# Attention's plan with a count of SP's transfer queue and new offsets, and a state factor from summed angles

## The chip, the cores and the metric

The kernel runs on one core of one Trainium2 chip. The metric is the device time of one execution in microseconds, as the median of several runs. The profile is one further execution of the same program, recorded by the hardware profiler; its span goes from the first to the last instruction.

The engines are called PE (TensorE, matrix products), DVE (VectorE), ACT (ScalarE), POOL (GpSimd) and SP (SyncE, which here only issues DMA transfers).

## What is computed

Three stages follow one another. A gated linear attention with a complex decay per channel, a mixture of experts with a greedy capacity-bound assignment, and a gated linear unit:

```python
# attention: B, H, S, D = 4, 8, 768, 48
mag = sqrt(a_re**2 + a_im**2)
scale = minimum(mag, 0.999) / (mag + 1e-6)
a_re_n, a_im_n = a_re * scale, a_im * scale
for t in range(S):                      # state S_re, S_im: D x D per head
    new_re = ar * S_re - ai * S_im
    new_im = ar * S_im + ai * S_re
    S_re, S_im = new_re + outer(k[t], v[t]), new_im
    y[t] = q[t] @ S_re
# experts: N, D, E, F = 3072, 384, 8, 1024; cap = N // E
#   tokens go to experts in the order of their logits, cap each
out[mask_e] = relu(x[mask_e] @ w1[e]) @ w2[e]
# unit: (x @ w_a) * (x @ w_b) @ w_out, 384 -> 1536 -> 384
```

## The kernel before

**Attention** works on chunks of 128 positions. There are 6 chunks and 4 batches; a pass (`i`, 0 to 11) handles one chunk `c = i // 2` of two batches at once, as tiles of 128 positions by 768 columns (two batches, eight heads, 48 channels). For each pass `gates` loads a_re, a_im, q, k and v and turns the decay into a logarithm `e` of its size and an angle `th`. `sums` forms the running sums along the chunk by matmul with a triangular matrix: `LL` for the sizes (with a rounded part `n` that VectorE computes and TensorE subtracts again) and `HH` for the angles, of which `r` keeps the part within one turn. `turned` takes sines of `r` (`s`, then squared, and `sn`) and turns k and q with them into `nat`. `unit` (one per batch) transposes `nat` (`TT`), forms the scores (`S`), the outer products of the state (`X`), the output (`Y`) and the router's logits (`O`).

The state passes from chunk to chunk through `factor`: for a pass `i` of two or more it builds, on 16 rows by 48 columns, the size and the cosine and sine of the turn from the last position of chunk `i - 2` to the last of chunk `i`. Its inputs are single rows of tiles, moved by SP into `fw` (lines 363 and 448): the last row of `s` and `sn` of pass `i - 2`, the first row of `s` and `sn` of pass `i`, the first row of `e` and `th`, and rows of `ea` into `ends`. Twelve VectorE instructions (lines 477 to 497) and three ScalarE instructions (469 to 473) make the factor; TensorE transposes it (line 503) and ScalarE copies it to `pb`. VectorE multiplies the state `xs` with it into `rta` and `rtb` (line 513), SP swaps the two halves of `rtb` into `sw` (two transfers, lines 517 and 518), and VectorE adds `rta` and `sw` to the state `Sb` (line 521). That state enters `Y` (line 587) and, with the outer product, the next `xs` (line 570).

**The order of the work** is fixed before the program is built, by `Plan`. Every step is a task with an engine, an assumed duration, what it reads and writes, and a due time (22 per pass). `order` lays the tasks out with a list scheduler: at each step it takes the engine and the task that can start earliest, and among those the one with the lowest rank. The rank is the due time times `STRETCH`, less the assumed length of the chain behind it in the same due time (`tail`), plus an offset `EARLIER` by kind (engine letter and name of the tile written, as `Sre` for SP's transfer of a_re or `Aln` for ScalarE's logarithm). A change of ScalarE's function table adds `SWITCH` to the rank and 1.3 us to the time, and is held back by `PATIENCE` while less than `ENOUGH` of work waits for that table. `land` is the time from the end of a transfer's issue to its landing:

```python
t["tail"] = t["dur"] + t["land"] + HOP[t["eng"]] + max(own, default=0.0)
t["rank"] = t["due"] * STRETCH - t["tail"] + EARLIER.get(t["kind"], 0.0)
```

The engines then run their instructions in that order and wait for each other by semaphores. SP issues its transfers in order too. The two pair banks of PSUM (`NPAIR = 2`) hold `LL`, `HH` and `TT`; `SPLIT_PAIRS` limits how many pairs `LL` and `HH` hold at once. `SINGLE = 1`: the first pass is done in two halves.

**Behind attention** the router (`make_router`, `route`, `lists`) assigns tokens to the first expert, and then `moe_glu` runs the eight experts with the unit, each expert's routing beside the products of the one before.

Of the kernel before, what the change touches and what calls it, by code (L numbers as in the profile page):

```python
# [16 lines left out]
OP = mybir.AluOpType  # L17
# [17 lines left out]
SWITCH = 61.0  # L35
# [12 lines left out]
PATIENCE = 7  # L48
ENOUGH = 21.5
# [7 lines left out]
class Plan:  # L57
# [8 lines left out]
    def add(self, eng, dur, fn, reads=(), writes=(), due=0.0, take=None, drop=None, table=None, land=0.0):  # L66
        t = dict(n=len(self.tasks), eng=eng, dur=dur * SLOW if eng == "P" else dur, fn=fn, due=due, take=take, drop=drop, table=table, land=land,
# [21 lines left out]
    def order(self):  # L89
# [30 lines left out]
        while any(waiting.values()):  # L120
# [71 lines left out]
def attention(tc, q, k, v, a_re, a_im, wg, x_dram, consts, L, guard, router, glu, late):  # L192
# [8 lines left out]
    with ExitStack() as st:  # L201
# [26 lines left out]
        for nm, x in (("one", 1.0), ("shift", LIFT), ("tiny", LN(2.0e-6)), ("quarter", HALF_PI)):  # L228
# [88 lines left out]
        def gates(i, due):  # L317
# [5 lines left out]
            load, land = (2.3, 2.2) if i < 2 else (0.6, 3.8)  # L323
            for us in parts(i):
# [3 lines left out]
                for nm, t, src in (("re", ld_re, a_re), ("im", ld_im, a_im)):  # L328
                    plan.add("S", took(load, us), lambda t=t, src=src, r=r, at=at, d2=d2: SP.dma_start(t[j][:, r], flat(src, at, d2)),
                             writes=[(nm, j, u) for u in us], due=due - 20 - 40 * (i < 2), land=land)  # L330
            for x, src in ((0, q), (1, k)):
                plan.add("S", load, lambda x=x, src=src: SP.dma_start(ld_qk[j][:, x], flat(src, base, dims)),
                         writes=[("qk", j, x)], due=due - 10, land=land)
            plan.add("S", load, lambda: SP.dma_start(vb[j].rearrange("p u h d -> p (u h) d")[:, :, 0:D], flat(v, base, dims)),
                     writes=[("v", j)], due=due - 4, land=land)
# [1323 lines left out]
```

## Time and profile before

| | us |
|---|---|
| median of 3 runs | 1066.19 |
| lowest, highest run | 1063.6, 1066.37 |
| the profiled execution | 1064.48 |
| its span | 1062.9 |
| PE busy, share of the span | 994.7 (94%) |
| DVE busy | 640.8 (60%) |
| ACT busy | 501.8 (47%) |
| POOL busy | 164.6 (15%) |
| mean granted clock of TensorE | 0.975 |

Busy times are sums over stages with different limits, so they don't tell what bounds a stage; the rows by stretch further down do. Attention fills roughly the first 287 us, and its share of DVE and ACT is far higher than that of the whole.

### The profile page before, as it was taken

How to read it: one execution, taken by the hardware profiler on the slowest of the kernel's cores; microseconds unless marked ns; L12 is line 12 of the kernel's file. 1: busy time of each engine (PE TensorE's matmuls, PEld its weight loads, DVE VectorE, ACT ScalarE, POOL GpSimd, SP SyncE). 2: the span in 40 equal slices, each digit the busy share in tenths (PEclk: the TensorE clock that was granted, in tenths of full speed). 3: DMA queues.
4: the chain of work that ended last, by engine and by line, in shares of the span. 5: the costliest groups of instructions: out<-in, count | busy, mean ns of one | idle time of the engine just before them, and what ended most of it. 6: DMA issues, size and time to landing. Idle time of an engine off the chain costs nothing. (4 is left out here: it accounts for less than half of the span.)

```text
span 1062.9 us, 17395 instructions
## 1 busy us (share of the span) xinstructions
PE 994.7 (94%) x6660; PEld 901.2 (85%) x6660; DVE 640.8 (60%) x1596; ACT 501.8 (47%) x906; POOL 164.6 (15%) x217
## 2 busy tenths in 40 slices
PE   3899999999987699999999999999999999999994
PEld 1588787888746599999989999999999999999994
DVE  4689888998677987555366355455536644333321
ACT  6799898887426773332332332243233234233221
POOL 6000000000021003203112120320311213102001
PEclk9999999999968789999999999999999999999998
DMA  9866777344145644102112110310211212201000
GB/s 170 129 120 124 121 130 135 74 89 111 42 140 166 177 143 127 53 8 96 33 38 79 42 45 1 105 52 8 90 35 42 69 47 78 76 15 45 1 2 26
DMA packets 146764, 81.90 MB, mean 77 GB/s; under 512 B 130416, under 2 KB 132336, under 8 KB 146672
## 3 DMA queue, kind: packets, MB, share of 16 engines
q1 hardware_dynamic: 134448, 41.36, 20.4%
q0 software_dynamic: 12224, 39.34, 11.6%
q8 instruction: 54, 0.88, 0.3%
q14 instruction: 38, 0.31, 0.1%
HBM read 68.04 MB, written 9.44 MB: 73 GB/s over the span
## 5 line engine op out<-in xcount | busy, mean ns | idle before, releaser
L1301 PE MATMUL mm<-yh,glu 128*128 128x384 f32 x1152 | 241.7, 344 | 0.0
L1301 PEld LDWEIGHTS mm<-yh,glu 128*128 128x128 f32 x1152 | 201.5, 189 | 2.1 <-ACT yh L1153 0.4
L1335 DVE TENSOR_TENSOR g<-mm,a_s 128x384 f32<-128x384 f32 x96 | 53.4, 556 | 154.7 <-PE mm L1301 130.4
L1301 PE MATMUL mm<-yl,glu 128*128 128x384 f32 x576 | 133.2, 338 | 0.0
L1153 ACT ACTIVATE gh<-g 128x384 fp32r<-128x384 f32 x96 | 50.4, 525 | 163.5 <-DVE g L1335 163.5
L1330 ACT ACTIVATE a_s<-mm 128x384 f32<-128x384 f32 x96 | 47.1, 491 | 151.1 <-PE mm L1301 142.7
L1301 PEld LDWEIGHTS mm<-yl,glu 128*128 128x128 f32 x576 | 103.4, 187 | 0.0
L1249 PE MATMUL acc<-glu,gh 128*128 128x384 f32 x288 | 98.4, 342 | 0.0
L1250 PE MATMUL acc<-glu,gh 128*128 128x384 f32 x288 | 96.9, 336 | 0.0
L1251 PE MATMUL acc<-glu,gl 128*128 128x384 f32 x288 | 96.7, 337 | 0.1
L1202 POOL DMA_INDIRECT raw<-moe_w_in,i x64 | 64.2, 1004 | 171.0 <-DVE w2l L1154 121.5
L1154 DVE TENSOR_TENSOR gl<-g,gh 128x384 fp32r<-128x384 f32 x96 | 53.6, 558 | 40.8 <-ACT gh L1153 39.9
L1250 PE MATMUL acc<-hl,w2h 128*128 128x384 f32 x192 | 67.0, 349 | 5.2 <-DVE hl L1276 5.2
L1249 PE MATMUL mm<-xh,w1h 128*128 128x384 f32 x192 | 67.4, 352 | 0.4 <-ACT w1h L1153 0.3
L1251 PE MATMUL acc<-hh,w2l 128*128 128x384 f32 x192 | 66.1, 344 | 0.0
L1251 PE MATMUL mm<-xh,w1l 128*128 128x384 f32 x192 | 65.1, 339 | 1.1 <-DVE w1l L1154 1.1
L1249 PE MATMUL acc<-hh,w2h 128*128 128x384 f32 x192 | 65.8, 353 | 0.2 <-ACT hh L1275 0.2
L1250 PE MATMUL mm<-xl,w1h 128*128 128x384 f32 x192 | 65.0, 339 | 0.0
L1188 POOL DMA_INDIRECT raw<-moe_w_in,i x24 | 24.2, 1008 | 253.1 <-DVE left L1062 172.5
L1153 ACT ACTIVATE w1h<-raw 128x384 fp32r<-128x384 f32 x64 | 32.7, 521 | 54.1 <-PE mm L1250 51.6
L552 PE MATMUL bank<-qkT 96*128 96x128 f32 x384 | 54.1, 286 | 3.7 <-ACT qkT L543 3.4
L1154 DVE TENSOR_TENSOR w1l<-raw,w1h 128x384 fp32r<-128x384 f32 x64 | 34.9, 552 | 36.3 <-ACT w1h L1153 29.8
(277 smaller groups left out, 2007.7 us busy)
## 6 DMA issues: line engine op xcount, KB each, us to landing
stage<-moe_w_a_in SPq DMA_DIRECT2D x13, 384.0 KB, 3.2
vb<-v_in SPq DMA_DIRECT2D x12, 384.0 KB, 5.0
ld_qk<-q_in SPq DMA_DIRECT2D x12, 384.0 KB, 4.3
ld_qk<-k_in SPq DMA_DIRECT2D x12, 384.0 KB, 5.8
x_rows<-xo POOLq DMA_DIRECT2D x24, 192.0 KB, 2.4
stage<-moe_w_b_in SPq DMA_DIRECT2D x12, 384.0 KB, 3.2
stage<-moe_w_out_in SPq DMA_DIRECT2D x12, 384.0 KB, 3.5
ld_im<-a_im_in SPq DMA_DIRECT2D x11, 384.0 KB, 5.9
```

Of the source, the lines that this page charges most:

```text
L552: PE.matmul(p[:, x], qt[0:96, 4 * h4 + x, 1], qt[0:96, 4 * h4 + x, 0], start=True, stop=True)
L1153: a = A.activation(hi, src, AF.Copy)
L1154: return a, V.tensor_tensor(lo_, src, hi, op=OP.subtract)
L1188: G.indirect_dma_start(out=raw[:, j], out_offset=None, in_=w1r, in_offset=bass.IndirectOffsetOnAxis(ap=i1[:, j:j + 1], axis=0))
L1202: G.indirect_dma_start(out=raw, out_offset=None, in_=w2r, in_offset=bass.IndirectOffsetOnAxis(ap=i2[:, f:f + 1], axis=0))
L1249: PE.matmul(p, lh, rh, start=first, stop=False)
L1250: PE.matmul(p, lh, rl, start=False, stop=False)
L1251: PE.matmul(p, ll, rh, start=False, stop=last)
L1301: PE.matmul(p, a[:, j, c], b[:, j], start=(n == 0), stop=(n == 8))
L1330: A.activation(a_s, pa, AF.Copy)
L1335: V.tensor_tensor(g, pb, a_s, op=OP.mult)
```

## The change

`Plan.add` takes a new argument `wire`: the time that a transfer keeps SP's queue busy behind its issue. `order` keeps one such clock for SP: a transfer is taken as sent when the earlier ones have left the queue, and its landing counts from there. Loads of the passes from 2 on have 2.0, those of the first two passes 0.0, swaps 0.4, the unit's weights 1.2, all others 0.1. `EARLIER`, `STRETCH`, `SWITCH`, `SPLIT_PAIRS`, `PATIENCE` and `ENOUGH` have new values.

The factor no longer takes rows of `s` and `sn` of both passes: it takes one row of `r` from each, adds the angles with that of `th`, brings the sum into one turn, and takes two sines of it. The twelve VectorE instructions become ten (`angle` 4, `size` 2, `three` 4), ScalarE's three stay three, and of four row transfers two remain. The bias `quarter` goes.

```diff
-SWITCH = 61.0
+SWITCH = 34
-SPLIT_PAIRS = 3
+SPLIT_PAIRS = 2
-EARLIER = {'Acc': -2, 'Ae': 99, 'Aea': 39, 'Afw': 11, 'Ag': -75, 'Aln': -20, 'Apb': -27, 'AqkT': 9, 'Arec': 15, 'As2': -5, 'Asf': -11, 'Ath': 58, 'Axo': 8, 'AyT': -36, 'G-': -59, 'GW': -21, 'Gconsts': 2, 'Gmasks': 51, 'Gzeros': -28, 'PF': -33, 'PHH': -2, 'PLL': -39, 'PO': 68, 'PS': -40, 'PTT': 90, 'PX': 59, 'PY': 126, 'Sends': 69, 'Sfw': 67, 'Sim': -99, 'Sqk': 72, 'Sraw': -57, 'Sre': 2, 'Ssw': -147, 'Sv': -41, 'V-': 19, 'VAb': -10, 'VS': 99, 'Ve': 29, 'Vearly': -29, 'Veb': 55, 'Vft': -4, 'Vg': -28, 'Vlg': 5, 'Vn4': -38, 'Vnat': -69, 'Vr': 33, 'Vrho': 89, 'Vrt0': -55, 'Vrt1': -13, 'Vsetup': -54, 'Vxs': -152}
-STRETCH = 3.699071
+EARLIER = {'Acc': 48, 'Ae': 17, 'Aea': -62, 'Afw': 2, 'Ag': 21, 'Aln': 213, 'Apb': -89, 'AqkT': -98, 'Arec': 89, 'As2': 53, 'Asf': 104, 'Asn': 73, 'Ath': 73, 'Axo': -339, 'AyT': -47, 'G-': -187, 'GW': 169, 'Gconsts': 370, 'Gmasks': 66, 'Gzeros': 230, 'PF': -31, 'PHH': -133, 'PLL': -104, 'PO': 106, 'PS': -2, 'PTT': -183, 'PX': -273, 'PY': 129, 'Sends': 36, 'Sfw': -102, 'Sim': 30, 'Sqk': -4, 'Sraw': 54, 'Sre': 20, 'Ssw': -293, 'Sv': 39, 'V-': -57, 'VAb': -23, 'VS': -129, 'Ve': 14, 'Vearly': -74, 'Veb': 138, 'Vft': -207, 'Vfw': 23, 'Vg': -26, 'Vlg': 5, 'Vn4': -181, 'Vnat': 18, 'Vr': 2, 'Vrho': 100, 'Vrt0': 101, 'Vrt1': 94, 'Vsetup': -169, 'Vxs': -26}
+STRETCH = 3.42
-PATIENCE = 7
-ENOUGH = 21.5
+PATIENCE = 8.0
+ENOUGH = 20.0
...
+        wire = 0.0
...
+            sent = end
+            if e == "S":
+                sent = max(end, wire)
+                wire = sent + t["wire"]
             for u in users[n]:
                 left[u] -= 1
-                ready_at[u] = max(ready_at[u], end + t["land"] + (HOP[e] if T[u]["eng"] != e else 0.06))
+                ready_at[u] = max(ready_at[u], sent + t["land"] + (HOP[e] if T[u]["eng"] != e else 0.06))
...
-            load, land = (2.3, 2.2) if i < 2 else (0.6, 3.8)
+            load, land, wire = (2.3, 2.2, 0.0) if i < 2 else (0.6, 3.8, 2.0)
...
-                row(fw[w][:, 0], ("fw", w, 0), s2, both(ks2), 127)
-                row(fw[w][:, 1], ("fw", w, 1), sn, both(ksn), 127)
+                row(fw[w][:, 0], ("fw", w, 0), r, both(kr), 127)
             if c:
                 w = i % 4
-                row(fw[w][:, 2], ("fw", w, 2), s2, both(ks2), 0)
-                row(fw[w][:, 3], ("fw", w, 3), sn, both(ksn), 0)
+                row(fw[w][:, 1], ("fw", w, 1), r, both(kr), 0)
...
-            plan.add("A", 0.22, lambda: A.activation(f[:, 4], f[:, 7], AF.Sin, bias=bias["quarter"][0:16]),
-                     [kf[7]], [kf[4]], table="T", **a)
-            plan.add("A", 0.22, lambda: A.activation(f[:, 5], f[:, 7], AF.Sin), [kf[7]], [kf[5]], table="T", **a)
...
+            def angle():
+
+                V.scalar_tensor_tensor(f[:, 0], f[:, 7], 0.5 / PI, f[:, 0], op0=OP.mult, op1=OP.add)
+                V.tensor_tensor(f[:, 0], f[:, 0], f[:, 1], op=OP.subtract)
+                V.tensor_scalar(f[:, 1], f[:, 0], TURN, TURN, op0=OP.add, op1=OP.subtract)
+                V.tensor_tensor(f[:, 0], f[:, 0], f[:, 1], op=OP.subtract)
+            plan.add("V", 0.86, angle, [kf[0], kf[1], kf[7]], [kf[0], kf[1]], **a)
+            plan.add("A", 0.22, lambda: A.activation(f[:, 3], f[:, 0], AF.Sin, scale=PI), [kf[0]], [kf[3]], table="T", **a)
+            plan.add("A", 0.22, lambda: A.activation(f[:, 2], f[:, 0], AF.Sin, scale=2 * PI), [kf[0]], [kf[2]], table="T", **a)
...
+            plan.add("V", 0.43, size, [kf[6], ("ends", i - 2, 0), ("ends", i, 1)], [kw], **a)
...
-            plan.add("V", 0.9, three, [kw, kf[6], ("ends", i - 2, 0), ("ends", i, 1)], [kw], **a)
+                V.scalar_tensor_tensor(f[:, 3], f[:, 3], 2.0, f[:, 3], op0=OP.mult, op1=OP.mult)
+                V.scalar_tensor_tensor(w[:, 8:10], f[:, 3, None].to_broadcast(sh), 1.0, w[:, 5, None].to_broadcast(sh),
+                                       op0=OP.subtract, op1=OP.mult)
+                V.scalar_tensor_tensor(w[:, 10], f[:, 2], -1.0, w[:, 5], op0=OP.mult, op1=OP.mult)
+                V.tensor_tensor(w[:, 11], f[:, 2], w[:, 5], op=OP.mult)
+            plan.add("V", 0.85, three, [kw, kf[2], kf[3]], [kw, kf[3]], **a)
...
-                plan.add("S", 1.15, swap, [("rt1", z)], [("sw", z)], land=2.4, **a)
+                plan.add("S", 1.15, swap, [("rt1", z)], [("sw", z)], land=2.4, wire=0.4, **a)
```

## Rows read from the trace of the kernel before

**Rows 1.** Busy time by stretch: from, to, length; busy time and instructions; clock; DMA.

```profile
15.56:51.00 35.44, 27.82 (x95) 16.61 (x96) 20.98 (x45) 24.54 (x39) 2.08 (x13) 1.00 1.10 153
...
82.74:103.69 20.95, 20.71 (x195) 18.16 (x194) 19.70 (x37) 19.74 (x31) 1.08 (x2) 1.00 0.72 129
103.69:128.07 24.38, 22.14 (x195) 18.91 (x194) 20.05 (x38) 19.91 (x30) 1.08 (x2) 0.93 0.73 127
128.07:149.61 21.54, 20.88 (x195) 17.51 (x195) 19.27 (x37) 19.23 (x28) 1.08 (x2) 1.00 0.69 126
149.61:172.01 22.40, 20.88 (x195) 17.51 (x195) 19.11 (x37) 19.23 (x28) 1.08 (x2) 1.00 0.67 121
172.01:193.78 21.77, 20.87 (x195) 17.51 (x194) 19.01 (x37) 19.24 (x28) 1.08 (x2) 1.00 0.60 107
193.78:213.32 19.54, 19.54 (x180) 15.82 (x179) 17.76 (x37) 18.30 (x26) 0.92 (x2) 1.00 0.44 89
```

**Rows 2.** The same for a late stretch, and the timeline's row of attention's last matmuls.

```profile
600.00:700.00 100.00, 100.00 (x608) 95.27 (x607) 52.22 (x147) 32.07 (x67) 18.77 (x19) 1.00 0.15 48
...
285.23 2.03 PE L600 MATMUL bank<-iw,yT 128*128 128x104 f32 x16
```

**Rows 3.** Waits of TensorE, 60 to 292 us: total, times, longest.

```profile
PE pair L375 <- DVE n L391: 6.7, 5, 2.2
```

**Rows 4.** Waits of VectorE, 60 to 292 us.

```profile
DVE Sb L521 <- DMA sw<-rtb: 8.3, 4, 2.8
```

**Rows 5.** Timeline, 107 to 117 us (start, length, instruction, idle); last: the swaps' issue (min/median/max).

```profile
107.89 2.96 SPq L517 DMA_DIRECT2D sw<-rtb  x1
...
113.73 0.56 DVE L521 TENSOR_TENSOR Sb<-rta,sw 96x384 f32<-96x384 f32 x1 [2.77 <-DMA sw<-rtb]
...
115.85 0.94 DVE L391 TENSOR_SCALAR n<-pair 128x768 bf16<-128x768 f32 x1
...
116.85 0.48 PE L375 MATMUL pair<-n,eye_minus 128*128 128x384 bf16 x2 [2.24 <-DVE n L391]
...
L517 SPq DMA_DIRECT2D sw<-rtb x20: 518/542/2956, 87.2 to 280.0; - x20
```

**Rows 6.** Busy time, 116 to 120 us, and TensorE's timeline: state matmuls there and later.

```profile
116.00:120.00 4.00, 3.15 (x34) 2.78 (x33) 4.00 (x5) 1.54 (x2) 0.00 (x0) 0.74 0.70 95
...
118.43 1.92 PE L587 MATMUL bank<-qkT,Sb 128*64 128x128 f32 x16
...
142.18 1.09 PE L587 MATMUL bank<-qkT,Sb 128*64 128x128 f32 x16
```

**Rows 7.** Timeline of the start, and DMA issues before 9 us (KB each, us to landing).

```profile
8.18 0.52 ACT L345 ACTIVATE ln<-ld_re 128x384 f32<-128x384 f32 x1 [5.95 <-DMA ld_re<-a_re_in]
...
9.39 0.56 DVE L352 TENSOR_TENSOR rho<-ld_im,rec 128x384 f32<-128x384 f32 x1 [6.38 <-ACT rec L345]
...
15.56 1.62 PE L375 MATMUL pair<-e,Ws 128*128 128x384 f32 x2 [15.56 <-DVE e L348]
...
0.95 1.84 SPq L329 DMA_DIRECT2D ld_im<-a_im_in  x3
...
ld_im<-a_im_in SPq DMA_DIRECT2D x2, 192.0 KB, 3.2
ld_im<-a_im_in SPq DMA_DIRECT2D x1, 384.0 KB, 5.0
```

**Rows 8.** Timeline: a factor's first and last VectorE instruction; groups by line and shape, 0 to 330.

```profile
272.82 0.19 DVE L477 TENSOR_SCALAR fw<-fw 16x96 f32<-16x96 f32 x1
...
275.14 0.19 DVE L497 SCALAR_TENSOR_TENSOR ft<-ft 16x48 f32<-16x48 f32 x1
...
L495 DVE TENSOR_TENSOR ft<-ft 16x96 f32<-16x96 f32 x10 | 2.5, 246 | 0.3
L471 ACT ACTIVATE fw<-fw,b_quarter 16x48 f32<-16x48 f32 x10 | 3.3, 332 | 1.5 <-DMA fw<-th 1.4
```

**Rows 9.** The same groups: ScalarE's table loads (count, busy time, mean ns).

```profile
L649 ACT ACT_TABLE_LOAD x23 | 29.5, 1283 | 0.4
```

More of the change, by code (lines that the diff above doesn't have):

```diff
@@ L64, in __init__, with add @@
         self.held, self.at_of = {}, {}
-    def add(self, eng, dur, fn, reads=(), writes=(), due=0.0, take=None, drop=None, table=None, land=0.0):
-        t = dict(n=len(self.tasks), eng=eng, dur=dur * SLOW if eng == "P" else dur, fn=fn, due=due, take=take, drop=drop, table=table, land=land,
+    def add(self, eng, dur, fn, reads=(), writes=(), due=0.0, take=None, drop=None, table=None, land=0.0, wire=0.1):
+        t = dict(n=len(self.tasks), eng=eng, dur=dur * SLOW if eng == "P" else dur, fn=fn, due=due, take=take, drop=drop, table=table, land=land, wire=wire,
                  after=set(), tail=0.0)
@@ L227, in attention @@
         bias = {}
-        for nm, x in (("one", 1.0), ("shift", LIFT), ("tiny", LN(2.0e-6)), ("quarter", HALF_PI)):
+        for nm, x in (("one", 1.0), ("shift", LIFT), ("tiny", LN(2.0e-6))):
             bias[nm] = cst.tile([128, 1], F32, name="b_" + nm)
@@ L329, in gates @@
                     plan.add("S", took(load, us), lambda t=t, src=src, r=r, at=at, d2=d2: SP.dma_start(t[j][:, r], flat(src, at, d2)),
-                             writes=[(nm, j, u) for u in us], due=due - 20 - 40 * (i < 2), land=land)
+                             writes=[(nm, j, u) for u in us], due=due - 20 - 40 * (i < 2), land=land, wire=wire)
             for x, src in ((0, q), (1, k)):
                 plan.add("S", load, lambda x=x, src=src: SP.dma_start(ld_qk[j][:, x], flat(src, base, dims)),
-                         writes=[("qk", j, x)], due=due - 10, land=land)
+                         writes=[("qk", j, x)], due=due - 10, land=land, wire=wire)
             plan.add("S", load, lambda: SP.dma_start(vb[j].rearrange("p u h d -> p (u h) d")[:, :, 0:D], flat(v, base, dims)),
-                     writes=[("v", j)], due=due - 4, land=land)
+                     writes=[("v", j)], due=due - 4, land=land, wire=wire)
             (ln, kln), (rec, krec), (rho, krho), (g, kg), (e, ke), (th, kth) = [
@@ L482, in factor @@
-            plan.add("V", 0.92, one, kf[0:4], [kw, kf[0], kf[2]], **a)
-            def two():
-                V.tensor_tensor(w[:, 0:4].rearrange("p (a b) d -> p a b d", a=2), w[:, None, 4:6].to_broadcast(sh),
-                                f[:, 4:6, None].to_broadcast(sh), op=OP.mult)
-                V.tensor_tensor(w[:, 6], w[:, 0], w[:, 3], op=OP.subtract)
-                V.tensor_tensor(w[:, 7], w[:, 1], w[:, 2], op=OP.add)
-            plan.add("V", 0.66, two, [kw] + kf[4:6], [kw], **a)
@@ L498, in factor @@
-            plan.add("V", 0.9, three, [kw, kf[6], ("ends", i - 2, 0), ("ends", i, 1)], [kw], **a)
+            sh = [2 * H, 2, D]
+            def angle():
[3 more added lines that the diff above has]
+                V.tensor_tensor(f[:, 0], f[:, 0], f[:, 1], op=OP.subtract)
@@ new lines, in factor, with size @@
+            plan.add("V", 0.86, angle, [kf[0], kf[1], kf[7]], [kf[0], kf[1]], **a)
+            plan.add("A", 0.22, lambda: A.activation(f[:, 3], f[:, 0], AF.Sin, scale=PI), [kf[0]], [kf[3]], table="T", **a)
+            plan.add("A", 0.22, lambda: A.activation(f[:, 2], f[:, 0], AF.Sin, scale=2 * PI), [kf[0]], [kf[2]], table="T", **a)
+            def size():
+                V.scalar_tensor_tensor(w[:, 4], ends[:, i - 2, 0], -math.exp(-2 * LIFT), ends[:, i, 1], op0=OP.mult, op1=OP.mult)
+                V.tensor_tensor(w[:, 5], w[:, 4], f[:, 6], op=OP.mult)
@@ L627, in attention @@
             kr, kw = ("raw", x % 2), ("word", x % 2)
-            plan.add("S", 0.6, (lambda x=x: glu.load(x)) if x else weights, [], [kr] + (taken if x == 0 else []), land=2.5, **end)
+            plan.add("S", 0.6, (lambda x=x: glu.load(x)) if x else weights, [], [kr] + (taken if x == 0 else []), land=2.5, wire=1.2, **end)
             if x == 0:
```

13 lines of the change are left out of this document (removed).

## The prediction

> **What bounds the kernel now.** I read the busy time by stretch first, cut at one and the same step of every pass of attention (the transpose of the factor), then the waits of TensorE and VectorE inside attention, then the timeline around the longest of those waits, and last the start. The chain of waits is of no help here: it ends in the last store and goes back no further.
>
> From about 400 us on TensorE has no gap: 100.00 of 100 us in a typical stretch [rows 2]. So the kernel is attention, then some 100 us of routing and first expert, then a stretch bound by TensorE that no edit touches. Attention's last matmuls start at 285.23 and take 2.03 us [rows 2], so it ends at 287.3; the remaining 1062.9 - 287.3 = 775.6 us I carry over unchanged. The question is where 287.3 goes.
>
> Inside attention TensorE is the bound too: outside the pass from 103.69 a pass has 20.7 to 20.9 us of matmul, VectorE 19.0 to 19.7 and ScalarE 19.2 to 19.7 [rows 1]. The pass from 82.74 takes 20.95 us, that from 193.78 has no gap at all, but the four between take 24.38, 21.54, 22.40 and 21.77 with the same 195 matmuls [rows 1]. At 20.95 each they would take 83.80 instead of 90.09: **6.3 us are lost there.** The waits name the place: TensorE waits for VectorE's n (the rounded sum of logarithms), 6.7 us in 5 waits [rows 3], and VectorE waits for the landing of sw, 8.3 us in 4 waits [rows 4]. The timeline of the worst pass joins the two [rows 5]: SyncE needs 2.96 us to issue one swap at 107.89, where the swap's median is 0.54; the swap's state add stands at the head of VectorE for 2.77 us; n is four instructions behind it, at 115.85; the matmul that reads n starts at 116.85 after 2.24 us of idling. So a transfer that is late in SP's queue becomes a gap of TensorE. After this gap the granted clock of the four microseconds is 0.74, a mixture of the two levels 1.2 and 2.4 GHz, and sixteen state matmuls take 1.92 instead of 1.09 us [rows 6].
>
> At the start, ScalarE's first logarithm waits 5.95 us for a_re, VectorE's first product starts at 9.39, TensorE's first matmul at 15.56 [rows 7]. Three loads of a_im (two of 192 KB, and the 384 KB of the second pass) are issued ahead of the first a_re.
>
> **The change part by part.**
>
> (1) *The plan counts SP's queue* (argument wire): a load of a later pass holds the queue 2.0 us, a row 0.1, a swap 0.4, and what follows lands that much later. It adds no instruction. It lets the planner see the delay shown in [rows 5], which it took for zero: in its old account a swap landed 2.4 us after its issue. The new plan also gives swaps more lead (Ssw from -147 to -293). I take the four sw waits as gone and with them the four passes' excess: **-6.3 us**. The ends: 0 if the delay is only put elsewhere; -6.3 for those passes. What is late next is TensorE itself: the gapless pass from 193.78 shows that it runs through with VectorE at 17.76 of 19.54 us [rows 1].
>
> (2) *The factor from the sum of angles.* VectorE's twelve instructions per factor, from 272.82 to 275.33 with one foreign one of 0.17 between [rows 8], become ten: nine of some 0.19 us and one of 0.25 by the nearest rows [rows 8], 1.96 against 2.34 us, about 0.4 us saved in each of 10 passes. ScalarE trades a sine with a bias (332 ns [rows 8]) for one without, which saves less than that a pass. The rows s2 and sn, four transfers in a middle pass, become one r out and one r in: 20 transfers fewer on SP. None of it lies on TensorE's path in a pass that TensorE fills, so I put it at nothing; the cover is the 1.2 us and more that VectorE and ScalarE have left per pass [rows 1]. If that cover were gone, VectorE's share would be worth 0.4 x 10 = 4 us. What moves matters more: the rows leave when r is there, before the two big sines rather than after them and their square, so factor, swap and state add can all be placed earlier. Two waits are added: the small sines now wait for angle on VectorE, behind the r rows; in ScalarE's order the copies for TensorE are queued behind them. And r, one buffer only, isn't rewritten until its row transfers have read it; the next writing is a pass (some 21 us) later, far more than the few microseconds of a landing, so I put this at nothing.
>
> (3) *The order at the start.* SP picks the lowest rank = due x STRETCH - tail + EARLIER. For the first pass's a_re and a_im, due and tail are the same, so EARLIER decides: Sre 2 against Sim -99 now, 20 against 30 after. With -99 even the second pass's a_im (due 22 later, 81 in rank) comes ahead of the first a_re. After, the order is a_re, a_re, a_im, a_im, then the second pass's. The first transfer of 192 KB lands some 3.2 us after its issue [rows 7], at 0.95 + 3.2 = 4.2, so the logarithm starts there instead of at 8.18. Then the product waits for a_im, third in line. The third now is 384 KB; it is issued behind two of 192 KB within 0.95 to 2.79 and takes 5.0 to land [rows 7]; issued at about 1.9 it lands at 6.9. A third of 192 KB is there by then. So the product starts by 6.9 instead of 9.39: **-2.5 us**, and the first matmul at about 13. I carry it to the end of the fill, since the fill is a chain of dependent steps (TensorE 27.82 of 35.44 us [rows 1]). Ends: all of the 7.6 us idle in that stretch could go besides (-10), or the new order of ScalarE could spend the gain and one set of gates more (five activations, about +4.5; nearest row the 0.52 us for half a tile [rows 7]).
>
> (4) *The refit* of EARLIER, STRETCH, SWITCH, PATIENCE, ENOUGH lays the whole of attention out anew. Every wait that the plan doesn't foresee is new. The four passes above had one each, 6.3 / 4 = 1.6 us each; I take one of that size to come back elsewhere: **+1.6 us**. Ends 0 and +6.3. SPLIT_PAIRS from 3 to 2 does nothing: there are two pair banks.
> SWITCH from 61 to 34 makes a change of ScalarE's table cheaper in the plan's eyes. A load takes 1283 ns and there are 23 of them [rows 9], two a pass; ScalarE has 20.95 - 19.2 = 1.7 us left per pass, so one more a pass costs TensorE nothing and two would. The Trainium skill, page "ScalarE: Activation LUTs", section "What ACT_TABLE_LOAD costs", speaks against the change here: it puts a switch at about 2.66 us, the load and as long again for a drain. By that a single extra load a pass would be too many and the sum would lose about 1 us a pass, some 10 us; the rows show the load alone.
>
> **Sum.** -6.3 - 2.5 + 1.6 = -7.2 us. The profiled execution took 1064.48 us (span 1062.9 and 1.6 around it) and would take 1057.3; against the median of the runs, 1066.19, which is 1.7 above the profiled one, it is **1059.0 us**.
>
> **The rivals.**
> *More goes* (the fill's 7.6 us idle shrinks by half beside the shift, no new wait): 1066.2 - 6.3 - 2.5 - 3.8 = 1053.6. For it: r's earlier rows loosen the state's chain; against: nothing in the trace shows that the idle of the fill comes from the order.
> *The stall moves*: the count is one constant per load, while issues in the trace vary from 0.54 to 2.96 us [rows 5]; swaps land in time but rows or loads stand late at VectorE's head, and the start's 2.5 us is all that stays, less one or two waits of 1.6: 1066.2 - 2.5 + 1.6 or 3.2 = 1065 to 1067. This is also what comes if the queue's account doesn't describe the chip.
> *Late gates, slower*: Aln goes from -20 to +213, some three passes' worth of rank (22 x 3.42 = 75 each). ScalarE takes the next pass's logarithms only when it has nothing else. Where they come late, TensorE waits at the sums LL for e or n, and a gap like that of [rows 5] with its clock costs 24.38 - 20.95 = 3.4 us [rows 1]. From three such passes on (10.2 against 8.8) the change loses; five give 1066.2 - 8.8 + 17 = 1074. For it: ScalarE has under 2 us left per pass; against: its idle time and the order by earliest start let waiting work in.
> *ScalarE's table, slower*: two extra loads a pass: 19.2 + 2.56 = 21.8 against 20.95, 0.8 x 10 passes = +8, with (3) 1072. It decides from 1.4 extra loads a pass.
>
> **How the numbers follow.** Forecast (1055 to 1063) 0.50, more goes 0.20, the stall moves 0.17, late gates 0.09, table 0.04. The likeliest is 1059.0. A measurement of this kernel can tell about 0.3%, 3.2 us, from no change. Faster by more: 0.70; within: 0.17; slower: 0.13. The range for 8 in 10 leaves out the deepest gains (start and idle of the fill both, under 1051) and most of the two slow cases: 1051 to 1069.
>
> **What would show it.** Right: no wait of Sb for sw above 1 us, hence none of TensorE for n beyond half a microsecond between 100 and 190; middle passes of 21 us at a clock of 1.00; first logarithm at about 4 us and first matmul at about 13; attention's last matmul ending near 280; 775 us behind it; about 24 table loads. Wrong: middle passes over 21.5 us whatever ends their waits (the stall moved); e, LL or n ending TensorE's idle in many passes (late gates); 36 or more table loads; a first matmul at 13 but the first gapless pass no earlier than now (the fill spent the gain); more than 778 us behind attention.

## The result and the profile after

| | before | after |
|---|---|---|
| median of 4 runs, us | 1064.89 | 1055.61 |
| lowest, highest | 1062.88, 1066.37 | 1054.47, 1056.2 |
| the profiled execution | 1064.48 | 1056.05 |
| its span | 1062.9 | 1054.5 |
| attention's last matmul ends | 287.3 | 277.6 |
| behind it | 775.6 | 776.9 |
| DVE busy, ACT busy | 640.8, 501.8 | 635.2, 499.8 |

The ratio is 0.9913, with a 95% interval from 0.989 to 0.9935. The forecast was 1059.0, with a range from 1051 to 1069. All of the gain lies in attention, which ends 9.6 us earlier.

The first view is the busy time by stretch, cut alike in both kernels at 60, 100 and 200 us and at attention's end (from, to, length; then busy time and instructions of PE, PEld, DVE, ACT and POOL; clock; DMA). Before:

```profile
0.00:60.00 60.00, 35.77 (x159) 22.88 (x159) 33.61 (x69) 41.13 (x66) 16.61 (x58) 1.00 1.04 146
60.00:100.00 40.00, 39.72 (x345) 33.81 (x346) 34.65 (x57) 39.07 (x56) 1.64 (x3) 1.00 0.71 128
100.00:200.00 100.00, 94.68 (x880) 80.10 (x878) 86.45 (x167) 86.12 (x126) 4.86 (x9) 0.98 0.64 115
200.00:287.30 87.30, 83.95 (x819) 72.00 (x817) 72.65 (x158) 66.52 (x98) 4.87 (x9) 1.00 0.37 84
```

After:

```profile
0.00:60.00 60.00, 38.02 (x229) 25.81 (x230) 39.47 (x77) 47.23 (x74) 17.89 (x59) 0.94 1.07 165
60.00:100.00 40.00, 38.98 (x354) 32.82 (x351) 35.41 (x66) 38.66 (x57) 1.62 (x3) 1.00 0.51 110
100.00:200.00 100.00, 97.24 (x898) 82.34 (x897) 87.69 (x163) 89.58 (x133) 4.87 (x9) 0.98 0.64 122
200.00:277.60 77.60, 73.37 (x726) 64.40 (x724) 58.61 (x122) 55.95 (x83) 4.32 (x8) 0.98 0.32 78
```

The reader is to see two things. By 60 us TensorE has run 229 matmuls instead of 159, with hardly more busy time: the fill has changed most. And TensorE's idle time falls from 5.32 to 2.76 us between 100 and 200, but rises from 0.28 to 1.02 before and from 3.35 to 4.23 behind.

Matmuls differ in length, so I put the same into microseconds: each matmul is weighed with the median distance to its successor among those of its form in the kernel before, from 60 to 275 us, where TensorE mostly runs at full speed. The time less the work done by then is the **lost time**; it holds idle time and the excess of matmuls that ran at half speed:

| us | 40 | 50 | 60 | 100 | 200 | 275 |
|---|---|---|---|---|---|---|
| before | 31.6 | 37.2 | 39.0 | 40.9 | 53.6 | 61.0 |
| after | 29.4 | 30.0 | 31.7 | 34.7 | 43.5 | 52.1 |

Of the 8.9 us gained by 275 us, 7.3 are gained in the first 60; 3.9 come between 100 and 200, and 1.1 and 1.2 are given back before and behind. These last two are no more than noise: a second build of the changed kernel (the last experiment) differs from this table by up to 1.2 us at a point. **So what the prediction took for the small term is the large one.**

Most of the fill's gain stands in one stretch: 2.2 us are gained by 40 us, and 5.0 more between 40 and 50. The window of these ten microseconds, before and then after:

```profile
40.00:50.00 10.00, 8.89 (x44) 7.53 (x43) 5.54 (x8) 6.61 (x8) 0.00 (x0) 1.00 0.82 121
```

```profile
40.00:50.00 10.00, 10.00 (x89) 8.51 (x87) 7.86 (x10) 9.97 (x14) 0.00 (x0) 1.00 1.06 177
```

TensorE is idle for only 1.1 of the 5.6 us that before loses there; the rest is matmuls at half speed. Before reaches full speed at 49.7 us, after at 39.4 (told by the length of known matmuls, see the last section). So the larger part of the gain in the fill comes where TensorE is at full speed earlier (in the second build 1.7 by 40 us and 4.5 from there to 50).

The start of after, from the timeline (start, length, engine, line, instruction; in brackets the idle time before it and what ended it), answers [rows 7]:

```profile
4.06 0.52 ACT L350 ACTIVATE ln<-ld_re 128x384 f32<-128x384 f32 x1 [1.83 <-DMA ld_re<-a_re_in]
...
6.24 0.63 DVE L357 TENSOR_TENSOR rho<-ld_im,rec 128x384 f32<-128x384 f32 x1 [3.84 <-DMA ld_im<-a_im_in]
...
9.04 0.60 ACT L350 ACTIVATE e<-g,b_tiny 128x384 f32<-128x384 f32 x1
9.55 0.83 ACT L350 ACTIVATE ln<-ld_re 128x768 f32<-128x768 f32 x1
...
10.38 1.62 PE L380 MATMUL pair<-e,Ws 128*128 128x384 f32 x2 [10.38 <-DVE e L353]
```

The logarithm starts at 4.06 instead of 8.18, the product at 6.24 instead of 9.39, the first matmul at 10.38 instead of 15.56. ScalarE makes the first e before the second pass's logarithm (the tile of 768). Before, it is the other way round:

```profile
11.79 0.83 ACT L345 ACTIVATE ln<-ld_re 128x768 f32<-128x768 f32 x1
...
13.86 1.10 ACT L345 ACTIVATE e<-g,b_tiny 128x384 f32<-128x384 f32 x2
```

The waits inside attention, 60 to 285 us (total, times, longest), answer [rows 3, 4]; TensorE first, then VectorE:

```profile
PE pair L380 <- DVE n L396: 2.5, 3, 1.8
PE pair L540 <- ACT qkT L543: 2.2, 4, 1.1
PE bank L552 <- ACT qkT L543: 2.0, 1, 2.0
PE bank L580 <- DVE Ab L554: 1.6, 1, 1.6
```

```profile
DVE fw L479 <- DMA fw<-r: 5.8, 3, 2.7
DVE ft L488 <- DMA ends<-ea: 5.1, 5, 1.4
...
DVE Sb L521 <- DMA sw<-rtb: 0.9, 4, 0.4
```

VectorE's wait for sw is gone (8.3 to 0.9), and TensorE's for n has fallen from 6.7 to 2.5. But new ones stand beside it: the rows listed make 8.3 us. The longest on TensorE is at 127.82, in a stretch at a granted clock of 0.64 (windows, then timeline):

```profile
127.00:131.00 4.00, 3.18 (x11) 2.58 (x12) 1.30 (x3) 3.97 (x7) 0.54 (x1) 0.64 0.98 223
```

```profile
121.72 0.53 SPq L334 DMA_DIRECT2D ld_im<-a_im_in  x1
...
122.34 1.50 SPq L368 DMA_DIRECT2D fw<-e  x1
...
126.25 0.24 ACT L472 ACTIVATE fw<-fw 16x48 f32<-16x48 f32 x1 [2.55 <-DMA fw<-e]
...
127.82 1.87 PE L552 MATMUL bank<-qkT 96*128 96x128 f32 x8 [1.96 <-ACT qkT L543]
...
131.77 1.06 PE L552 MATMUL bank<-qkT 96*128 96x128 f32 x8
```

It is the gap of [rows 5, 6] over again, one engine on: a row of e for the factor is issued behind a load of a_im, its issue takes 1.50 us, ScalarE stands 2.55 us for it, the copy qkT behind it is late, and TensorE idles for 1.96 us; then the same eight matmuls take 1.87 instead of 1.06 us. The pass around it is the longest (same columns as above, cut at the factor's transpose, answering [rows 1]):

```profile
109.10:134.37 25.27, 23.15 (x207) 19.39 (x205) 20.29 (x39) 20.04 (x31) 1.08 (x2) 0.93 0.71 138
134.37:155.30 20.93, 20.80 (x196) 17.34 (x194) 18.25 (x34) 18.92 (x27) 1.08 (x2) 1.00 0.56 112
```

### The profile page after: what moved, and what is told of

The parts are those of the page before. It is cut to its first block, busy times and chain, and to the rows that moved or that the text cites. A ratio compares the mean times of both kernels' runs of the same rounds, so it can differ in the third digit from the quotient of the medians.

```text
span 1054.5 us, 17312 instructions
## 1 busy us (share of the span) xinstructions
PE 987.8 (94%) x6660; PEld 897.8 (85%) x6660; DVE 635.2 (60%) x1575; ACT 499.8 (47%) x906; POOL 164.8 (16%) x217
## 4 chain that ended last, share of the span: by engine, by line
PE 79%; DVE 7%; DMA 6%; ACT 4%; issue 2%; POOL 1%; another core or an unknown queue 0%; SPq 0%; POOLq 0%; DVEq 0%; ACTq 0%
PE mm L1301 28%; PE acc L1249 8%; PE acc L1250 8%; PE acc L1251 8%; PE pair L380 4%; PE mm L1249 3%; PE mm L1251 3%; PE mm L1250 3%; PE pair L540 2%; PE bank L552 2%; DMA ends<-ea 2%; PE bank L563 2%; PE bank L580 2%; PE bank L600 1%; PE bank L587 1%
## 5 line engine op out<-in xcount | busy, mean ns | idle before, releaser
L1154 DVE TENSOR_TENSOR gl<-g,gh 128x384 fp32r<-128x384 f32 x96 | 53.6, 558 | 40.7 <-ACT gh L1153 36.9
L1153 ACT ACTIVATE w1h<-raw 128x384 fp32r<-128x384 f32 x64 | 32.7, 521 | 54.6 <-PE mm L1250 52.2
L1251 PEld LDWEIGHTS acc<-glu,gl 128*128 128x128 f32 x288 | 54.0, 188 | 1.2 <-DVE gl L1154 1.1
```

What stands on the lines that cost most here:

```text
L1153: a = A.activation(hi, src, AF.Copy)
L1154: return a, V.tensor_tensor(lo_, src, hi, op=OP.subtract)
L1251: PE.matmul(p, ll, rh, start=False, stop=last)
```

## The experiments

Attention's end is given for each, against 287.3 before and 277.6 after; it is the end of the last row of attention's last matmuls (line 600 before), in one profiled execution. The ratios are to 10, 13 or 26 further runs of the kernel before, taken beside each experiment; the 49 of them have a median of 1063.6. Four versions of the kernel before whose medians are no faster end attention 0.5 to 2.0 us earlier than 287.3, so a difference of that size tells nothing.

**The loads' order in the fill, alone.** In the kernel before, only the first six loads of SP are put into the order of after:

```diff
-        for at, n, table in self.order():
+        for at, n, table in loads_first(self, self.order()):
+    loads.sort(key=lambda o: (T[o[1]]["due"], T[o[1]]["kind"] == "Sim", o[1]))
```

> Kernel before, but the first six loads are issued in the new order (a_re, a_re, a_im, a_im of the first pass, then a_re and a_im of the second); all other orders are as before. Theory of the prediction: first logarithm at 4.1, first product by 6.9, first matmul at about 13 instead of 15.56, attention's end 2.5 us earlier, 284.8. Rival A (the fill multiplies it: TensorE comes to its high clock earlier, and the ten microseconds that it works at half speed around 40 to 50 us shrink): 5 us or more. Rival B (the fill is held by something later, such as ScalarE's order or the loads of q and k): under 1 us.

Measured: ratio 1.0006 (0.9995 to 1.0017), attention's end 286.2. The timeline:

```profile
13.35 1.62 PE L375 MATMUL pair<-e,Ws 128*128 128x384 f32 x2 [13.35 <-POOL qkT L291]
...
33.73 0.84 ACT L345 ACTIVATE ln<-ld_re 128x768 f32<-128x768 f32 x1 [3.87 <-DMA ld_re<-a_re_in]
...
35.00 0.48 PE L375 MATMUL pair<-n,eye_plus 128*128 128x384 bf16 x1 [2.66 <-ACT sf L394]
```

The first matmul comes at 13.35, as the prediction's step (3) worked out, but the old order of ScalarE has a later pass's logarithm ahead of sf; its load now lands too late for the quicker fill, and TensorE waits 2.66 us. At most 1.1 us remain, and that isn't clear of noise.

**The loads' order taken back, alone.** The changed kernel with the old order of the first six loads:

```diff
+    loads.sort(key=lambda o: (T[o[1]]["kind"] != "Sim", T[o[1]]["due"], o[1]))
```

> Changed kernel, but the first six loads are issued in the old order (three a_im ahead of the first a_re); all else as changed. Theory of the prediction: 2.5 us slower, attention's end at 280.1. Rival A (the start is worth more because it also decides when TensorE reaches its high clock, 39 us in the changed kernel against 50.6 before): 5 us or more, high clock after 44 us. Rival B (ScalarE's new order is what made the start fast): first matmul still before 13, under 1 us lost.

Measured: ratio to before 0.9949 (0.9931 to 0.9966), attention's end 281.5; first matmul at 14.01. With the run above this makes a square of attention's end: neither 287.3, loads alone 286.2 (-1.1), the rest of the change without the loads 281.5 (-5.8), both 277.6 (-9.6). The lost time at 60 us in the same order: 39.0, 37.9, 34.0, 31.7. **In the fill, the loads' order is worth at most 1.1 alone and some 2.3 with the rest of the change; the rest is worth 5.0 without it.** The rest is more than the engines' order: it holds the new factor, TensorE's earlier full speed (43.4 us here), and the order of SP's other loads, since after issues the first q and k at 6.87 and 8.85 us, where before issues v at 6.68 and q and k only at 13.39 and 15.69. The square doesn't tell these apart.

**The first pass first.** If the order of the engines carries the fill, the plain reading of it is that the first pass goes ahead of the second. In the kernel before, with the new load order, every first-pass step of ScalarE, VectorE and TensorE is put right behind what it needs:

```diff
+        for at, n, table in first_pass_first(self, self.order()):
...
+        if t["due"] != PERIOD or t["eng"] not in "AVP":
+            continue
...
+        low = max([out.index(x) for x in out[:at] if x[1] in t["after"]], default=-1) + 1
...
+        out.insert(low, o)
```

> The kernel before; the first six loads in the order a_re, a_re, a_im, a_im and then the second pass's, and every step of the first pass is put right behind the steps that it needs on ScalarE, VectorE and TensorE (so the second pass's logarithm falls behind the first pass's sf, cc and ea). All else as before. Theory A (the fill is worth about 7 us, and the order of all engines in it carries the gain, not the loads alone): first matmul near 10.5 to 13, TensorE at full speed about 10 us earlier than before, attention ends 5 to 8 us earlier (280 to 283), run 1057 to 1060. Theory B (the rest of the plan gives it back, as with the loads alone): the wait for sf near 35 goes but VectorE or ScalarE stand at another step of the second pass; attention ends less than 2 us earlier, run 1062 to 1065.

Measured: ratio 1.0243 (1.0216 to 1.0269), attention's end 310.2. Both theories fell. TensorE's waits in the first 85 us, and the busy time of 20 to 40 us:

```profile
PE pair L375 <- ACT th L345: 11.7, 2, 6.4
PE pair L375 <- DVE e L348: 10.1, 1, 10.1
```

```profile
20.00:40.00 20.00, 8.45 (x24) 4.80 (x24) 7.92 (x18) 8.32 (x14) 0.00 (x0) 1.00 0.82 114
```

With one pass ahead of all else the engines take turns: none of them is busy for half of these 20 us, and the lost time at 80 us is 61.7 instead of 40.1. One reserve goes with this: the edit leaves ScalarE's table changes where the old order has them, so the first pass's th still stands behind the second pass's logarithm, and TensorE waits 6.4 us for it, until 22.50. What a first pass would give that takes its table change along isn't tested. What after has is a mixture: the first e ahead of the second pass's logarithm, the rest interleaved.

**Loads behind the swaps.** In the kernel before, loads of later passes that SP would issue within 10 us (by the plan) ahead of a swap go behind it, if their first reader comes later still. Nothing else moves:

```diff
+        for at, n, table in loads_behind(self, self.order()):
+        for x in [x for x in out[:p] if x[1] >= 0 and T[x[1]]["kind"] in ("Sre", "Sim", "Sqk", "Sv") and o[0] - x[0] < 10.0]:
...
+            if last > p:
+                out.insert(out.index(o) + 1, x)
```

> Kernel before; only SyncE's order is changed: where no reader is in the way, loads of later passes (mostly a_im) that stood ahead of a pass's swaps are issued behind them (this holds in three of the four slow passes, not in that from 128.07, where a_im and v stay ahead; v stays ahead everywhere). TensorE, VectorE and ScalarE keep their order. The swaps on GpSimd's queue were issued in time and still landed late (median 3.8 us), so the delay seems to be in the DMA engines that loads and swaps share. Theory (the loads' bytes ahead of a swap make it late, and that costs TensorE its gap): swap to landing under 3.5 us in those passes, VectorE's waits for sw down from 8.3 to about 3, the passes from 103.69, 149.61 and 172.01 near 21 us, attention's end 4 to 5.7 us earlier than 287.3. Rival (something else is late right behind, so that a swap in time gains nothing): waits for sw gone, attention's end within 1.5 us.

Measured: 1058.67 us, ratio 0.9948 (0.9929 to 0.9966), attention's end 281.4, 5.9 earlier. Waits of VectorE and TensorE from 60 us on, and four passes:

```profile
DVE Sb L521 <- DMA sw<-rtb: 4.4, 5, 1.5
...
PE pair L375 <- DVE n L391: 3.0, 3, 1.4
```

```profile
103.40:124.92 21.52, 20.53 (x195) 17.46 (x195) 19.45 (x38) 19.92 (x30) 1.08 (x2) 1.00 0.80 144
124.92:146.41 21.49, 20.87 (x195) 17.51 (x194) 19.79 (x38) 19.11 (x28) 1.08 (x2) 1.00 0.69 126
146.41:167.13 20.72, 20.72 (x195) 17.52 (x195) 19.12 (x38) 19.13 (x28) 1.08 (x2) 1.00 0.67 131
167.13:187.84 20.71, 20.71 (x195) 17.52 (x195) 18.55 (x36) 19.24 (x28) 1.08 (x2) 1.00 0.56 113
```

The passes of 24.38, 21.54, 22.40 and 21.77 [rows 1] take 21.52, 21.49, 20.72 and 20.71, 84.44 us instead of 90.09. The prediction's 6.3 us for this term was right within what the runs tell (5.5 us by the medians, with an interval from 3.6 to 7.6), and the term is to be had without any other part of the change.

The same edit was put on top of the first-pass-first order, to see whether the two stretches add:

> The kernel before with both edits to its order: the fill of the run above, and SP's order with loads of later passes behind the swaps (which alone moved attention's end by -6.0). No constant, no cost and no factor of the change is in it. If the two gains stand in different stretches and add (theory A): attention ends 11 to 14 us earlier, at 273 to 276, run about 1051 to 1054, and it beats the changed kernel. If the second is what the first needs or gives back (theory B): 278 to 281, run 1056 to 1059.

Measured: 1085.04 us, ratio 1.0178 (1.0149 to 1.0207), attention's end 305.9: far from a version that beats the changed kernel, since the fill is spoilt. Against the same fill without it, though, attention ends 4.3 us earlier, with VectorE's sw waits at 4.2 us in 5. So the worth of the swaps' lead hangs little on the fill.

**Is it SP's queue, or what lies behind it?** In the kernel before, GpSimd issues the swaps, so that they stand behind no load:

```diff
-                    SP.dma_start(sw[z][0:48], rt1[z][48:96])
+                    G.dma_start(sw[z][0:48], rt1[z][48:96])
```

> Kernel before, but the swaps of rtb into sw are issued by GpSimd on its own queue instead of SyncE; the order of TensorE, VectorE and ScalarE is the same instruction by instruction. Theory of the prediction (late swaps cost the four middle passes 6.3 us): VectorE's waits for sw fall from 8.3 to under 2 us, TensorE's for n from 6.7 to about 1.4, the passes from 103.69 take about 21 us, attention ends at 281 instead of 287.3, the run is about 6 us faster. Rival (the swap is only the first of several late inputs; the next one stands at VectorE's head as soon as it is gone, or GpSimd's transfers are later still): attention ends within 1.5 us of 287.3.

Measured: ratio 1.0013 (0.9996 to 1.003), attention's end 285.5. The worst pass of [rows 5] again, from the timeline, and VectorE's wait (60 to 290 us):

```profile
106.71 0.52 POOL L517 DMA_DIRECT2D sw<-rtb  x1 [5.36 <-DVE rtb L513]
...
113.37 0.56 DVE L521 TENSOR_TENSOR Sb<-rta,sw 96x384 f32<-96x384 f32 x1 [2.88 <-DMA sw<-rtb]
```

```profile
DVE Sb L521 <- DMA sw<-rtb: 9.9, 6, 3.2
```

No issue takes over 0.53 us now, and the swaps are issued by 108.75; VectorE stands for them as long as before. The swaps' transfers (KB, median us to landing) from 100 to 180 us, where loads are issued, and from 258 to 281, behind the last loads; this kernel and then before:

```profile
sw<-rtb POOLq DMA_DIRECT2D x16, 72.0 KB, 5.1
sw<-rtb POOLq DMA_DIRECT2D x8, 72.0 KB, 2.0
```

```profile
sw<-rtb SPq DMA_DIRECT2D x16, 72.0 KB, 2.4
sw<-rtb SPq DMA_DIRECT2D x8, 72.0 KB, 2.2
```

GpSimd's swaps are no slower as such: 2.0 us without loads. Among loads they take 5.1. SP's hardly land later among loads (2.4 against 2.2); they are held up before that, at their own issue in the worst pass [rows 5], and in the three other late passes at the row transfer `ends<-ea` between a load and the swap, whose issue takes 1.91, 3.08 and 1.94 us. What was lost at SP's issue comes back as a longer landing. Which of the resources behind the queues the loads and swaps share isn't shown; that GpSimd's queue doesn't help is.

Both edits of the kernel before at once, new load order and swaps by GpSimd:

> Both edits on the kernel before: swaps on GpSimd's queue and the new order of the first six loads. If the two places are independent the gains add up: 6.3 + 2.5 = 8.8 by the prediction, attention's end at 278.5, about that of the changed kernel (277.6), without a new plan and without the new factor. If they are not, about the larger of the two alone, within 2 us.

Measured: ratio 1.0018 (1.0001 to 1.0035), attention's end 285.3, first matmul at 13.10, VectorE's sw waits 9.5 us. The misses add up to a miss.

**The factor alone.** The kernel before, in its old order, with the new instructions; the first pass's row of r, `angle` and the small sines are placed as the expectation says:

```diff
-                row(fw[w][:, 2], ("fw", w, 2), s2, both(ks2), 0)
-                row(fw[w][:, 3], ("fw", w, 3), sn, both(ksn), 0)
+                row(fw[w][:, 1], ("fw", w, 2), r, both(ks2), 0)
-                V.tensor_scalar(f[:, 0:3:2], f[:, 0:3:2], -1.0, 1.0, op0=OP.mult, op1=OP.add)
+                V.scalar_tensor_tensor(f[:, 0], f[:, 7], 0.5 / PI, f[:, 0], op0=OP.mult, op1=OP.add)
```

> The kernel before with the new factor in the old order: one row of r instead of rows of s and sn (the first pass's row leaves right behind r), angle on VectorE at the start of ScalarE's stretch of sines, the two small sines 1.5 us behind it; size, the rest of the factor and all other steps stay where they were. Term (2) of the prediction (0): run within 2 us of before, attention ends 285 to 289, Sb's waits for sw as before (8 us), VectorE 4 us less busy. Rival (the factor itself carries a part of the gain, by 20 fewer transfers on SP or shorter VectorE work): attention ends 3 us or more earlier. Rival (the added wait costs): VectorE stands at angle for the landing of r and the run is 3 us or more slower.

The row of r that leaves the first pass for the third does so here while r is written anew, so one factor has another angle; all instructions and transfers are there.

Measured: ratio 1.0007 (0.9994 to 1.002), attention's end 286.7. VectorE is busy for 635.7 us, 5.1 less than before. Its waits for sw (60 to 292 us):

```profile
DVE Sb L517 <- DMA sw<-rtb: 7.8, 5, 2.5
```

The factor's instructions are worth nothing in the old order, as term (2) said. Whether its earlier rows helped the new order isn't told by this.

**The account and the constants, one without the other.** The changed kernel with the queue's clock off, then with the old constants:

```diff
-                wire = sent + t["wire"]
+                wire = sent
```

> Changed kernel, but the planner's account of SP's queue is switched off (a transfer counts as sent at the end of its issue, as before); constants and factor as changed, so attention is laid out anew. Theory of the prediction (the account is what takes the swaps out of VectorE's way): waits for sw, or for the rows of r, of 5 us and more come back in the stretch from 60 us on and attention ends 3 to 6 us later than 277.6. Rival (the new constants, above all the order at the start, carry the gain whatever the account says): within 2 us of 277.6.

> Changed kernel with the old SWITCH, SPLIT_PAIRS, EARLIER, STRETCH, PATIENCE and ENOUGH; the account of SP's queue and the new factor stay, attention is laid out anew. Theory from the two traces (7 of the 9 us were gained before 60 us, by the order at the start, which EARLIER sets): the gain is gone, attention ends at 285 or later and the run is no faster than before. Theory of the prediction (the account and the factor take 6.3 us out of the middle): attention ends near 281.

Measured: 1081.0 us without the account, ratio 1.0179 (1.0149 to 1.021), attention's end 305.6; 1071.76 us with the old constants (1064.65 to 1075.55), ratio 1.0092 (1.0063 to 1.0121), attention's end 289.3 in the execution of 1064.65, VectorE's sw waits 9.9 us in 7. Without the account ScalarE stands at the factor for rows; with the account and the old constants VectorE stands for sw as before:

```profile
ACT fw L472 <- DMA fw<-e: 14.2, 5, 4.3
```

```profile
DVE Sb L521 <- DMA sw<-rtb: 9.9, 7, 3.9
```

Without the account, no wait of VectorE for sw is among the rows, but VectorE and ScalarE stand for rows of the factor. So the new offsets, with the swaps' lead (Ssw at -293) among them, take the swaps out from behind the loads, and the account by itself doesn't; as far as these two runs show, the account keeps the rows from taking their place. Neither alone is a gain, and the constants were chosen under the account, so what each part is worth can't be read from these two.

The version with the old constants tells something of the fill too. TensorE's steps are those of before, and the lost time at 35 us is the same 28.9, but full speed comes at some 36 us instead of 49.7. The first eight transposes, in this kernel and before:

```profile
39.01 1.04 PE L540 MATMUL pair<-ident,nat 128*96 128x128 f32 x8
```

```profile
40.29 1.92 PE L540 MATMUL pair<-ident,nat 128*96 128x128 f32 x8
```

At 50 us it has lost 32.7 instead of 37.2, at 60 us 34.7 instead of 39.0. **So an earlier full speed is worth some 4 us in the old fill**, without the new loads' order and offsets. The new factor, which this version also has, doesn't bring it by itself (49.9 us in the run with the factor alone). What made it come early isn't shown; it is one execution, the fastest of its four, and behind the fill it loses more than before.

**A warm TensorE.** Since TensorE comes to full speed some 10 us earlier in after, I gave the changed kernel products with no use, 110 before the first and 5 behind each step of TensorE until the first transposes:

```diff
+                PE.matmul(plan.banks[5][:, 0:128], warm, warm, start=True, stop=True)
```

> Changed kernel with extra products on TensorE that nothing reads: 110 small bf16 products (128x128 by 128) ahead of attention's first matmul, where TensorE idles until 10.4 us, and five behind each of its steps until the first transpose. Theory (the fill is worth so much because TensorE works at half speed in it, and comes to full speed at 39 us in the changed kernel, at 50.6 before): full speed from the first matmul on or soon after, matmuls of the fill half as long, attention's end 2 us earlier or more than 277.6. Rival (the fill is a chain of ScalarE, VectorE and loads that a faster TensorE doesn't shorten): first gapless stretch at the same time, attention's end within 1 us; extra products in the way could cost up to 1 us.

Measured: ratio to before 0.9947 (0.9929 to 0.9966), attention's end 279.9. The first sum, from the timeline:

```profile
10.45 0.88 PE L390 MATMUL pair<-e,Ws 128*128 128x384 f32 x2 [0.36 <-DVE e L363]
```

It takes 0.88 us instead of the 1.62 of after, but the speed doesn't last: from 27.8 to 40.3 us TensorE is at half speed again (granted clock 0.50 from 30 to 40), and reaches full speed for good at 40.7, later than after. The lost time is 23.4 instead of 24.4 at 30 us, 29.6 instead of 29.4 at 40 and 32.0 instead of 31.7 at 60. So speed in the first 27 us gave 1.0 us here, and that is gone by 40; what full speed is worth from 27 to 40 us this run doesn't tell. That attention ends 2.3 us later than after comes behind 200 us and isn't explained.

**A small change of the layout.**

```diff
-STRETCH = 3.42
+STRETCH = 3.43
```

> The changed kernel with STRETCH 3.43 instead of 3.42, a change of 0.3% in the weight of the due times and nothing else. If a layout's time is a matter of its parts (theory A), attention ends within 1 us of 277.6 and the run is 1055 to 1057. If each layout is one draw from many and the fit has picked a good one (theory B), new waits of 1 to 2 us come up at other places and the run is 1058 or more; then the runs with one constant or the account turned off tell of the fit and not of a part's worth.

Measured: 1055.99 us, attention's end 277.2. The order came out the same on TensorE, ScalarE, GpSimd and SP; on VectorE one memset of 0.07 us and one e changed places at about 28 us. So this is all but a second build of the changed kernel, and tells neither theory: it shows that attention's end repeats within 0.4 us. The lost time doesn't repeat as well: 29.9, 31.0, 32.0, 35.9, 44.4 and 51.8 us at the six points of the table, so differences of 1.2 us between two of them tell nothing. How far the result hangs on the fit of the constants stays open.

## Why the prediction was right, step by step

**What bounds the kernel** held: the stretch behind attention is as long as before (776.9 against 775.6; over all runs here it lies between 771.9 and 777.7, which no run explains), and the time went where the waits of [rows 3 to 6] had pointed, though not only there.

**Term (1), -6.3**: mechanism and size right. The waits for sw are gone (0.9 us in all, the longest 0.4), and moving loads behind the swaps alone gave 5.9 us. That it is SP's *queue* was too narrow: swaps from GpSimd's queue, which carries no load, were as late. The remedy is the same, since it keeps the loads away from the swaps in time. The new offsets were needed for it: with the account and the old constants the waits for sw were 9.9 us.

**Term (2), 0**: right (+0.7 us, within the interval of no change). The saving on VectorE was worked out as 0.4 us a pass, 4 in all; 5.1 were measured. The waits that it added on VectorE (5.8 us for r's rows) cost TensorE little; whether nothing isn't shown, since the longest, 2.69 us up to 252.49, stands ahead of TensorE's gap of 1.57 us at 258.42 (waiting for VectorE's Ab), with VectorE idle for only 0.40 us between. That r's earlier rows let the state come earlier wasn't tested by itself.

**Term (3), -2.5**: the failed size. Its steps up to the product were right (4.06 for 4.2; 6.24 for at most 6.9), and loads alone gave the first matmul at 13.35 for "about 13". But the sentence that carries those 2.5 us to the end of the fill, "since the fill is a chain of dependent steps", failed in both directions. With the old order of the engines at most 1.1 remained. With the new one the first matmul came 5.2 us earlier, of which 1.0 was left at 30 us and 2.2 at 40; then 5.0 more came between 40 and 50 us, where before runs at half speed and after at full speed. So the size that failed is the fill's: 7.3 measured for 2.5, because the prediction priced it in idle time and put TensorE's speed in it at nothing. With the old constants an earlier full speed gave some 4 us. Why it comes earlier in after is open. The prediction also missed what the new offsets do to the order of ScalarE: the second pass's logarithm goes behind the first e, as Aln at +213 would have it, an offset that it had looked at only as a danger for later passes (late gates), where it did no harm. No run moves that step alone, so how much of the gain hangs on it isn't shown. (The end of +4.5 for five activations would be 5.2 by the row named, ten halves of 0.52; nothing hangs on it.)

The end of -10 that it gave for the fill was the nearer one. The rival "more goes", 1053.6, is nearer to the 1055.61 measured than 1059.0, but only by the high starting point that both have (see the sum below): its -12.6 is further from the measured -8 to -9 than -7.2. Nor does its mechanism hold: by 60 us TensorE's idle time fell by only 2.2 us (38.02 busy instead of 35.77; by 4.5 in the second build), and new waits did come.

**Term (4), +1.6**: undersized. From 60 to 275 us the lost time fell from 22.0 to 20.4, so if the 6.3 us of term (1) were had in full, some 4.7 came back (4.1 by the second build of the changed kernel): 1.96 us for qkT at 127.82, the rest in shorter waits and at the lower clock behind them. This is worked out by subtraction; no run shows it by itself. One wait was expected, several came; the end of +6.3 covered it. The rival "the stall moves" came true in this one place: behind a load, a row was late instead of a swap.

So the sum of -7.2 stands beside -8.4 in the profiled execution (-9.3 by the medians of the first table, -8.0 from 1063.6) partly by luck, because the two misses have opposite signs: 7.3 instead of 2.5 gained in the fill, 4.7 instead of 1.6 given back behind it. The 1055.61 lies 3.4 us under the 1059.0, and most of that is the starting point: the 1066.19 of three runs lies 2.6 above the 1063.6 of the 49 further runs, from which -7.2 gives 1056.4. "Middle passes of 21 us at a clock of 1.00" was wrong for the pass from 109.10 (25.27 us at 0.93, with 207 matmuls in it).

**Late gates** and **ScalarE's table** stayed away: after has the same loads as [rows 9], from the groups by line:

```profile
L649 ACT ACT_TABLE_LOAD x23 | 29.5, 1283 | 0.4
```

As no load was added, no run here tells what a further one would cost, and the 2.66 us that the Trainium skill gives for a switch ("ScalarE: Activation LUTs", section "What ACT_TABLE_LOAD costs") stays untried. The rows at hand look otherwise: a load has 1283 ns, with 0.4 us of idle time in front of all 23 together, and the next instruction of ScalarE starts 11 to 12 ns behind each, so no drain of a load's length is to be seen.

## What to carry to other kernels

A small transfer that an engine waits for was late here because of the large ones issued shortly before it; GpSimd's queue didn't cure that, issuing the large ones behind it did, and the excess of the passes over the gapless one was a fair price for it. When every offset of a planned order is refitted, lay out the first pass engine by engine from the new ranks before you price the fill, price its matmuls at the speed that they have there (here half of the later one, for the first 40 or 50 us), and expect new waits for much of what you take away (4.7 of 6.3 us here). The account and the constants fitted under it were a gain only together: test such parts together, and test single causes by moving single steps of a fixed order.

## What was not expected of the hardware

**A swap behind loads is late, whoever issues it**: from SP it is held at the issue (2.96 us in the worst pass, with 0.54 in the median) and lands in a median of 2.4 us; from GpSimd the issue stays at 0.5 us, and the landing takes 5.1 us among loads and 2.0 without them.

**Matmuls at half speed while the row of the clock reads 1.00.** In the kernel before, eight transposes take 1.91 us at 46.46 and 1.04 at 53.49 (timeline); the granted clock of 40 to 50 us reads 1.00 (window shown in the section on the result):

```profile
46.46 1.91 PE L540 MATMUL pair<-ident,nat 128*96 128x128 f32 x8
...
53.49 1.04 PE L540 MATMUL pair<-ident,nat 128*96 128x128 f32 x8
```

After, the same eight take 1.91 at 36.10 and 1.04 at 42.65, and there the row does show it: the granted clock of 36 to 38 us reads 0.50. So in the fill a row of 1.00 is no proof of full speed; the length of a known matmul tells.
